# Nine groups of tiles per run of q times k^T v, with one slot in a lent PSUM bank, and k^T v joined to the first run of a later batch

## The chip, the cores and the metric

The kernel runs on one core of one Trainium2 chip. The metric is the device time of one execution in microseconds (us), the median of several runs. "Profiled execution" is one more execution, recorded instruction by instruction; every duration below comes from it.

## The reference, cut to what matters

Linear attention without softmax, an RMS norm, and a gated feed-forward layer, all in float32:

```python
kv  = einsum('bhsd,bhse->bhde', k, v)        # 8 batches, 8 heads, 576 positions, 64 wide
out = einsum('bhsd,bhde->bhse', q, kv)
x   = out / sqrt(mean(out * out, -1) + 1e-6) * g_norm     # then (B,H,S,D) -> (4608, 512)
y   = (1 / (1 + exp(-(x @ w_gate))) * (x @ w_val)) @ w_out  # 512 -> 1536 -> 512
```

`moe_w_gate`, `moe_w_val`, `moe_w_out` arrive as float64 and are converted on the chip.

## The kernel before

**Feed-forward part.** The 4608 rows are nine chunks of 512. Chunk 0 is multiplied plainly (L599, L833). In this time the weights are converted on VectorE and ScalarE in steps named CV (L197 to L237), five to a unit of weights, and a unit of w_out must be ready before the matmuls of L833 that read it. Chunks 1 to 8 use a fast scheme: per chunk 3 x 26 "products" of 128x128 by 128x256 for the first layer (L957, two matmuls to a product) and 26 for the second (L1059). Products go into five PSUM banks, handed out by the queue `free` and returned by `give`. A bank is a *region* with a letter (A to K): several products accumulate into it one after the other, and between them its value is read out, by ScalarE where a step says "o5=A" (L923), by VectorE where it adds (L927). So the next product into a letter waits for the step that reads it out. In the first layer the products 0 to 8 of each third go into A, B, C, E, A, C, B, A, C; "o5=A" stands behind product 3, "o4=C" behind 4, "o3=B o1=A" behind 5.

**Attention part.** Batch 0 is done ahead by `attention`. Batches 1 to 7 are done by `feed(b)` in small steps set between the matmuls of the feed-forward part. For each batch:

- `kv_mm` computes k^T v for all eight heads: 32 matmuls of 128 rows by 64 columns (L389, "mains", positions 0 to 511) and eight of 64 by 64 (L396, "tails", the last 64 positions); `kv_copy` brings the result to `kvq` on ScalarE (L404, L405).
- `turn` transposes q on VectorE (L408, L410) into `qTs`.
- A *run* (`heads_run(m)`, m = 0, 1) is four heads. Its `u_mm` multiplies q by k^T v in 64x64 tiles (L439), four at a time: two halves of the rows of the array (heads g) by two halves of its columns (heads e). Then on ScalarE the square (L444, "sq") and the root (L450), sums on VectorE (L447), the norm, and transposes and DMAs of the result to `xT_ring`.

A run has nine slots for each g. Eight slots fill a PSUM bank, so g = 0 writes the first bank of the tile `at` (three banks, one buffer), g = 1 the second, and both ninth slots lie in the third. Before, the last slot of g = 1 is computed from the other half of the rows, so that the two halves never write one bank together. That takes a second copy of half of k^T v (L405), a second load of the last slots of q (L120) and their transposes (L410), and it makes ten groups: eight with four matmuls, two with two.

A matmul of float32 shows in the trace as two passes, each with a weight load: a run is 36 matmuls and 72 passes.

**Order.** Steps sit at positions: in chunk 0 by the table `places` (88 matmuls; "au" is `u_mm` of batch 1's first run, "bu" of its second, asq and bsq their squares, as0 a sum, LL2 the loads of batch 2's k and v, KV2 its `kv_mm`, ASIDE the copy that frees `at`, D its `kv_copy`); in the chunks 1 to 6 by `where`, position 26 j + i for product i of third j ("25:u0" is `u_mm` of run 0 behind product 25, "54:u1" that of run 1, "56:q1" its square). Every engine works through its own instructions in this order. ScalarE also issues DMAs: of LL2 and of the later k and v loads the four of the last 64 positions (L139).

Of the kernel before, what the change touches and what calls it, by code (L numbers as in the profile page):

```python
# [20 lines left out]
def kernel(  # L21
# [11 lines left out]
    nc = tc.nc  # L33
# [20 lines left out]
    JR = S // QB  # L54
    NSL = JR // 2
    NRUN = NHP // 2
    QW = 2 * S + 2 * HD

    NK4 = S // P
    S4 = P * NK4  # L60
# [44 lines left out]
    def load_q_run(b, m):  # L105
        if b >= B:
            return
        if b == 1:
            t = h_main[2 - m].rearrange("p s c -> p (s c)")[:, 4 * NT * P - QW:4 * NT * P]
        else:  # L110
            t = sb.tile([P, QW], FP32, tag="q", name="q", bufs=1)
        main = t[:, 0:2 * S].rearrange("p (e j c) -> p e j c", e=2, c=QB)
        more = t[:, 2 * S:QW].rearrange("p (e j c) -> p e j c", e=2, c=QB)
        queue = nc.gpsimd if b == 1 else nc.sync
        for i in range(NC):
            for e in range(2):
                for g in range(2):
                    src = q[b, 4 * m + 2 * g + e].rearrange("(p j) d -> p j d", j=JR)[:, :, QB * i:QB * i + QB]
                    queue.dma_start(out=main[HD * g + QB * i:HD * g + QB * i + QB, e], in_=src)
                queue.dma_start(out=more[QB * i:QB * i + QB, e], in_=src[:, JR - 2:JR])  # L120
        q_late[b, m] = t

    kv_late = {}
# [142 lines left out]
    g_col = const.tile([P, 1], FP32, name="g_col")  # L266


    kvq = const.tile([P, 2, NRUN, 2, HD], FP32, name="kvq")
    kv_ahead = const.tile([P, NRUN, 2, HD], FP32, name="kv_ahead")  # L270

    qTs = const.tile([P, QW], FP32, name="qTs")
# [17 lines left out]
    def attention(n, at_ps):  # L290

        b, m = divmod(n, NHP)
        d = {}
        kv = kvq[:, 0, m // 2, m % 2]

        def kv_mm():
            d["kv"] = ps = at_ps("kv")
# [78 lines left out]
    def feed(b):  # L376

        d = {}

        def kv_mm():  # L380

            mains, rest = kv_late[b]
            d["kv"] = ps = at_ps()[:, 0:NRUN, 0:2 * HD].rearrange("p m (e d) -> p m e d", d=HD)
            for m in range(NRUN):
                for e in range(2):
                    for j in range(NK4):
                        for g in range(2):
                            c = slice(NK4 * HD * e + HD * j, NK4 * HD * e + HD * j + HD)
                            nc.tensor.matmul(ps[HD * g:HD * g + HD, m, e], mains[2 * m + g, "k"][:, c],  # L389
                                             mains[2 * m + g, "v"][:, c],  # L390
                                             start=(e == 0 and j == 0), stop=False, skip_group_check=True)
            for e in range(2):
                for m in range(NRUN):
                    for g in range(2):
                        rs, c = slice(PH * m, PH * m + PH), HD * (2 * g + e)
                        nc.tensor.matmul(ps[HD * g:HD * g + HD, m, e], rest[rs, c:c + HD],  # L396
                                         rest[rs, GH + c:GH + c + HD], start=False, stop=True, skip_group_check=True)

        def kv_set_aside():
            nc.scalar.copy(out=kv_ahead, in_=d["kv"])  # L400
            d["kv"] = kv_ahead

        def kv_copy():
            nc.scalar.copy(out=kvq[:, 0], in_=d["kv"])  # L404
            nc.scalar.copy(out=kvq[0:HD, 1], in_=d["kv"][HD:P])  # L405

        def turn(m, e):
            nc.vector.transpose(qTs[:, S * e:S * e + S], q_late[b, m][:, S * e:S * e + S])  # L408
            if e == 1:
                nc.vector.transpose(qTs[0:HD, 2 * S:QW], q_late[b, m][0:HD, 2 * S:QW])  # L410
                if b > 1:
                    load_q_run(b + (m + 1) // NRUN, (m + 1) % NRUN)
                elif m == NRUN - 1:
                    load_q_run(b + 1, 0)

        def heads_run(m):
# [6 lines left out]
            def place(g, s_):  # L423
                return (NSL - 1) * g + s_ if s_ < NSL - 1 else 2 * (NSL - 1) + g
# [2 lines left out]
            def by_head(t):  # L427
                return t.rearrange("p (n d) -> p n d", d=HD)

            def u_mm():  # L430
                d["u"] = u = at_ps().rearrange("p r c -> p (r c)")[:, 0:2 * S]
                for t in range(NSL + 1):
                    for g in range(2):
                        if t < NSL - 1 or g == 0:
                            head, s_ = (1, NSL - 1) if t == NSL else (g, t)
                            o = HD * place(head, s_)
                            for e in range(2):
                                c = 2 * S + HD * e if t == NSL else S * e + HD * s_
                                nc.tensor.matmul(u[HD * e:HD * e + HD, o:o + HD],  # L439
                                                 qTs[HD * g:HD * g + HD, c:c + HD],  # L440
                                                 kvq[HD * g:HD * g + HD, t == NSL, m, e], start=True, stop=True)

            def u_square():
                nc.scalar.activation(out=sq, in_=d["u"], func=AF.Square)  # L444
# [43 lines left out]
            return ([u_mm, u_square, lambda: u_sum(0), lambda: u_sum(1), u_root] + norms +  # L488
                    [lambda i=i: x_turn(i) for i in range(NC)])

        kv = [kv_mm, kv_copy, kv_set_aside] if b == 2 else [kv_mm, kv_copy]
        t0, t1 = ([lambda m=m, e=e: turn(m, e) for e in range(2)] for m in range(NRUN))
        u0, u1 = heads_run(0), heads_run(1)
        if b == 1:
            return kv, t0 + t1 + u0 + u1, ()
        n_ = "n{0}0 n{0}1 n{0}2 n{0}3 n{0}4 n{0}5 n{0}6" if b == 2 else "n{0}0 n{0}1"
# [1 line left out]
        steps_ = dict(zip(names, t0 + t1 + u0 + u1[:-2]))  # L498
        where = """0:t00 5:t01 25:u0 26:q0 28:t10 30:s00,s01 33:t11 35:r0 36:n00 37:n01 39:n02 40:n03 42:n04 43:n05 44:n06
                   51:x00 52:x01 53:u1 56:q1 57:s10,s11 60:r1 62:n10,n11 63:n12 65:n13 66:n14 68:n15 69:n16""" if b == 2 else """  # L500
                   5:t00 8:t01 28:u0 29:t10 30:q0 33:s00,s01 36:r0 39:t11 41:n00 47:n01 51:x00,x01 54:u1
                   56:q1,s10,s11 61:r1 64:n10 66:n11""" if b == 3 else """
                   3:t00 7:t01 28:u0,t10 30:q0,s00,s01 37:r0 39:t11 47:n00,n01 53:x00,x01 54:u1
                   56:q1,s10,s11 60:r1 61:n10 63:n11"""
        first = [(int(w_.split(":")[0]), steps_[x]) for w_ in where.split() for x in w_.split(":")[1].split(",")]
        return kv, first, u1[-2:]
# [53 lines left out]
    def bank(i):  # L560
        return (psum_mm if i < 2 else psum).tile([P, 512], FP32, tag=f"mm{i}", name="mm")
# [6 lines left out]
    def at_ps():  # L568
        return psum.tile([P, NAT, 512], FP32, tag="at", name="at")
# [212 lines left out]
    def w1_form(c, j, part, v):  # L782
        if c == 1:
# [10 lines left out]
    w1_more[1] = [more[:, i] for i in range(10, 18)] + [sgs[-1][:, GH * i:GH * i + GH] for i in range(2)]  # L794
    spare_sg = sgs.pop()
    batch1, second_batch = feed(1), feed(2)
    named = {"LL": lambda: load_late(1), "LL2": lambda: load_late(2), "KV": batch1[0][0], "KV2": second_batch[0][0],
             "W0": lambda: w1_sums(0), "W1": lambda: w1_sums(1),
             "ASIDE": second_batch[0][2], "CV": convert_step}
    named.update({"C": batch1[0][1], "D": second_batch[0][1]})  # L800
    for i in range(NRUN):
        named[f"Q{i}"] = lambda i=i: load_q_run(1, i)
        named.update({f"t{i}{e}": batch1[1][2 * i + e] for e in range(2)})
    for i, which in enumerate("ab"):
        for n, step in enumerate(("u", "sq", "s0", "s1", "rt", "rc", "n0", "n1", "n2", "x0", "x1")):
            named[which + step] = batch1[1][2 * NRUN + 11 * i + n]
    places = """
        1:CV,CV 2:CV,Q0 4:CV,CV 5:CV,CV 6:CV,LL 7:CV,CV 10:CV,CV 11:Q1 15:CV 16:CV,CV 17:t00
        18:CV,CV 19:t01 20:KV 22:CV,CV,C 25:CV 26:CV,CV 29:au,LL2 30:CV
        31:asq 32:CV,t10,as0 34:CV,as1,art 35:CV 36:t11,arc,an0 37:an1 38:CV,an2 40:CV,CV 41:CV,ax0  # L810
        43:ax1 44:KV2,ASIDE 46:CV,W0 47:bu 48:CV,CV,bsq 50:CV,bs0 52:CV,CV 54:bs1 55:CV,CV,brt,D 57:CV,CV 58:CV 60:CV,brc
        62:bn0,bn1 63:bn2 64:CV 65:CV,CV,CV 66:CV,CV 67:CV 71:bx0 72:CV 74:W1 75:bx1
        80:CV,CV,CV,CV,CV 84:CV 87:CV,CV
    """
# [317 lines left out]
    for c in range(1, NG):  # L1132
        at1, at2 = {}, {}
        for p, step in x_late:
            at1.setdefault(p, []).append(step)
        x_late = []
        if c + 1 < B:
            kv, first_, then = second_batch if c == 1 else feed(c + 1)
            for p, step in (list(zip((21, 22) if c == 2 else (19, 20), kv)) if c > 1 else []) + first_:
                at1.setdefault(p, []).append(step)  # L1140
            for p, step in zip((3, 6) if c == 1 else (4, 6), then):
                at2.setdefault(p, []).append(step)
        if c + 1 < NG:
            for n, p in enumerate(X1 if c == 1 else X2 if c + 1 < B else X3):
                step = lambda n=n, c=c: x_sum(c + 1, n)
                if p < NPR:
                    at2.setdefault(p, []).append(step)
                else:
                    x_late.append((p - NPR, step))
        if c == 1:  # L1150
            for at_, forms in ((at1, ((28, 9, 0), (30, 10, 0), (34, 12, 0), (52, 11, 1), (57, 14, 0), (58, 8, 1), (61, 19, 0), (64, 16, 1))), (at2, ((1, 13, 0), (2, 22, 0), (3, 23, 1), (4, 25, 1), (9, 15, 0), (10, 24, 0), (10, 20, 0), (11, 17, 0), (12, 18, 0), (13, 21, 0)))):
                for p, n, pool_ in forms:
                    at_.setdefault(p, []).append(lambda n=n, eng=nc.gpsimd if pool_ else nc.vector, at_once=at_ is at1 or n == 13: w_form(n, eng, at_once))
        first_layer_fast(c, at1)
        if c == 1:
            sgs += [spare_sg] + more_sgs
        second_layer_fast(c, at2)
# [30 lines left out]
```

## Time and profile before

| | us |
|---|---|
| median of three runs (1003.74 to 1005.06) | 1004.05 |
| profiled execution | 1004.44 |
| its span, first to last instruction | 1002.7 |
| outside the span (difference of the two) | 1.7 |
| PE busy | 993.8 (99%) |
| DVE busy | 722.1 (72%) |
| POOL busy | 617.5 (62%) |
| ACT busy | 342.5 (34%) |

PE is TensorE's matmuls, DVE VectorE, ACT ScalarE, POOL GpSimd; PEld are weight loads. The granted TensorE clock is 1.0. In the chain of waits and in the timeline each line is a start, a length, and an engine with the line of the kernel; square brackets tell how long the engine idled before and what released it.

### The profile page before, as it was taken

How to read it: one execution, taken by the hardware profiler on the slowest of the kernel's cores; microseconds unless marked ns; L12 is line 12 of the kernel's file. 1: busy time of each engine (PE TensorE's matmuls, PEld its weight loads, DVE VectorE, ACT ScalarE, POOL GpSimd, SP SyncE). 2: the span in 40 equal slices, each digit the busy share in tenths (PEclk: the TensorE clock that was granted, in tenths of full speed). 3: DMA queues.
4: the chain of work that ended last, by engine and by line, in shares of the span. 5: the costliest groups of instructions: out<-in, count | busy, mean ns of one | idle time of the engine just before them, and what ended most of it. 6: DMA issues, size and time to landing. Idle time of an engine off the chain costs nothing.

```text
span 1002.7 us, 16624 instructions
## 1 busy us (share of the span) xinstructions
PE 993.8 (99%) x5958; PEld 815.8 (81%) x5958; DVE 722.1 (72%) x1198; ACT 342.5 (34%) x606; POOL 617.5 (62%) x988
## 2 busy tenths in 40 slices
PE   8999999999999999999999999999999999999998
PEld 7455447888888888888888888888888888888887
DVE  4989999889757756784677676866587566755672
ACT  4566332562144213530344124421342133213320
POOL 1509997798359633965186707861595449744963
PEclk9999999999999999999999999999999999999999
DMA  9995414673799568846875577755864555444514
GB/s 271 269 265 183 172 51 115 215 236 127 248 301 272 176 189 240 239 156 203 257 240 171 181 223 237 203 171 179 258 201 141 167 173 211 156 149 162 214 53 122
DMA packets 156114, 195.43 MB, mean 195 GB/s; under 512 B 84832, under 2 KB 128864, under 8 KB 156032
## 3 DMA queue, kind: packets, MB, share of 16 engines
q0 software_dynamic: 22000, 114.11, 34.4%
q1 hardware_dynamic: 126864, 78.16, 27.6%
q10 hardware_dynamic: 7168, 2.10, 0.9%
q8 instruction: 47, 0.77, 0.3%
q14 instruction: 35, 0.29, 0.1%
HBM read 160.50 MB, written 25.56 MB: 186 GB/s over the span
## 4 chain that ended last, share of the span: by engine, by line
PE 73%; POOL 2%; DMA 1%; issue 0%; SPq 0%; DVE 0%; POOLq 0%
PE mm L957 46%; PE mm L1059 24%; PE at L439 1%; POOL h L733 1%; PE at L389 1%; DMA h_more<-in_v_dram 1%; POOL w_ring L1030 0%; POOL h_more L733 0%; PE at L396 0%; SPq L134 0%; POOL w L780 0%; DVE sg L927 0%; POOLq L780 0%; POOLq L1030 0%
## 5 line engine op out<-in xcount | busy, mean ns | idle before, releaser
L957 PE MATMUL mm<-xs,w 128*128 128x256 f32 x1428 | 331.8, 380 | 0.0
L957 PEld LDWEIGHTS mm<-xs,w 128*128 128x128 f32 x1428 | 270.5, 190 | 37.1
L957 PE MATMUL mm<-xT,w 128*128 128x256 f32 x948 | 229.8, 380 | 0.0
L957 PEld LDWEIGHTS mm<-xT,w 128*128 128x128 f32 x948 | 179.5, 190 | 25.0 <-issue 0.5
L780 POOL DMA_DIRECT2D w<-kept x84 | 46.8, 557 | 189.4 <-PE mm L957 187.3
L927 DVE TENSOR_TENSOR sg<-sg,mm 128x512 f32<-128x512 f32 (+1 forms) x176 | 100.7, 599 | 85.5 <-PE mm L957 41.5
L1059 PE MATMUL mm<-w,h 128*128 128x256 f32 x630 | 143.1, 379 | 0.3 <-POOL h L733 0.3
L1059 PEld LDWEIGHTS mm<-w,h 128*128 128x128 f32 x630 | 119.6, 190 | 17.0 <-POOL h L733 0.7
L919 POOL TENSOR_TENSOR h<-h,sg 128x512 f32<-128x512 f32 x72 | 96.0, 1350 | 57.0 <-DVE h L927 31.0
L923 ACT COPY temps<-mm 128x512 f32<-128x512 f32 (+1 forms) x128 | 66.0, 538 | 186.9 <-PE mm L1059 94.7
L733 POOL TENSOR_TENSOR h<-h 128x128 f32<-128x128 f32 x216 | 112.1, 531 | 16.6 <-DVE h_more L733 13.1
L1059 PE MATMUL mm<-w,h_more 128*128 128x256 f32 x474 | 108.2, 379 | 0.0
L916 ACT ACTIVATE sg<-sg 128x512 f32<-128x512 f32 x96 | 59.7, 630 | 131.5 <-DVE sg L927 131.5
L1059 PEld LDWEIGHTS mm<-w,h_more 128*128 128x128 f32 x474 | 90.1, 190 | 12.2
L923 ACT COPY sg<-mm 128x512 f32<-128x512 f32 (+1 forms) x112 | 56.9, 510 | 86.5 <-PE mm L1059 45.0
L733 POOL TENSOR_TENSOR h_more<-h 128x128 f32<-128x128 f32 x120 | 61.6, 517 | 34.3 <-DVE h L919 30.0
L927 DVE TENSOR_TENSOR temps<-temps,mm 128x512 f32<-128x512 f32 (+1 forms) x96 | 59.4, 619 | 25.9 <-PE mm L1059 16.6
L599 PE MATMUL mm<-xT,w 128*128 128x512 f32 x176 | 77.8, 596 | 0.1
L927 DVE TENSOR_TENSOR temps<-mm,temps 128x512 f32<-128x512 f32 (+1 forms) x64 | 39.8, 622 | 50.9 <-PE mm L1059 23.6
L923 ACT COPY h<-mm 128x512 f32<-128x512 f32 x48 | 28.1, 585 | 140.4 <-PE mm L957 126.4
L927 DVE TENSOR_TENSOR sg<-mm,sg 128x512 f32<-128x512 f32 (+1 forms) x64 | 39.7, 620 | 45.1 <-PE mm L957 24.5
L599 PEld LDWEIGHTS mm<-xT,w 128*128 128x128 f32 x176 | 32.6, 190 | 39.2 <-issue 36.8
(145 smaller groups left out, 1284.2 us busy)
## 6 DMA issues: line engine op xcount, KB each, us to landing
w<-kept POOLq DMA_DIRECT2D x42, 896.0 KB, 5.7
w<-kept POOLq DMA_DIRECT2D x90, 384.0 KB, 4.6
w<-kept POOLq DMA_DIRECT2D x42, 768.0 KB, 5.5
out_dram<-sg SPq DMA_DIRECT2D x119, 64.0 KB, 1.7
h_more<-in_k_dram SPq DMA_DIRECT2D x28, 256.0 KB, 5.6
h_more<-in_v_dram SPq DMA_DIRECT2D x28, 256.0 KB, 6.5
q<-in_q_dram SPq DMA_DIRECT2D x96, 72.0 KB, 5.0
xT<-xTs SPq DMA_DIRECT2D x96, 72.0 KB, 4.4
```

The source lines that it names most:

```text
L389: nc.tensor.matmul(ps[HD * g:HD * g + HD, m, e], mains[2 * m + g, "k"][:, c], mains[2 * m + g, "v"][:, c], start=(e == 0 and j == 0), stop ...
L439: nc.tensor.matmul(u[HD * e:HD * e + HD, o:o + HD], qTs[HD * g:HD * g + HD, c:c + HD], kvq[HD * g:HD * g + HD, t == NSL, m, e], start=True ...
L599: nc.tensor.matmul(self.ps[i], w[("wg", "wv")[i], self.f][:, m, :], xT[self.c][:, m, :], start=(m == 0), stop=(m == NMT - 1), skip_group_c ...
L733: ops.append((eng, lambda v=v, x=x, sign=sign, y=y, eng=eng: eng.tensor_tensor(out=h_form(v, j), in0=h_form(x, j), in1=h_form(y, j), op=op ...
L780: nc.gpsimd.dma_start(out=granule(g)[:, 0:n], in_=kept1[g // NPA % N3, g % NPA][:, 0:n])
L916: nc.scalar.activation(out=o["o" + step[1]], in_=o["o" + step[1]], func=AF.Sigmoid)
L919: mult.tensor_tensor(out=o[x], in0=o[x], in1=o[y], op=ALU.mult)
L923: nc.scalar.copy(out=o[out_], in_=o[expr])
L927: tt(out=o[out_], in0=o[x], in1=o[y], op=ALU.add if sign == "+" else ALU.subtract)
L957: nc.tensor.matmul(regions[name][1][:, g], ws[:, g], xf[c][wv], start=(new and g == 0), stop=True, skip_group_check=True)
L1059: nc.tensor.matmul(regions[name][1], h_form(hv, j), ws[:, j], start=(used[i] and j == 0), stop=(j == N3 - 1), skip_group_check=True)
```

## The change

- `u_mm` takes a bank out of `free` (bank 4 in chunk 0) for the ninth slot of g = 1. The run then has nine groups of four matmuls, all of the same form. Behind them ScalarE copies the slot, 128x64, from the lent bank to its place in `at`, and the bank is given back.
- The second copy of k^T v, the second loads of q (four DMAs of twelve per run) and their transposes go.
- For batches 3 to 7, `kv_mm` and `kv_copy` no longer stand at products 19 and 20 (21 and 22 for batch 3), nor u0 at 28: all stand behind product 25, in one go. k^T v of run 0 lies in the third bank of `at`, that of run 1 in the lent bank. The tails come first, then the mains of run 0, then those of run 1; each half has a copy of its own.
- Batch 2's `kv_mm` joins "bu" in the same way, at 44 of chunk 0; bu was at 47. Its copy aside is two copies and moves from 44 to 47, behind bsq, which moves from 48 to 47.

```diff
-    QW = 2 * S + 2 * HD
+    QW = 2 * S
...
-                queue.dma_start(out=more[QB * i:QB * i + QB, e], in_=src[:, JR - 2:JR])
...
-        def kv_mm():
+        def kv_mm(at, lent):
             mains, rest = kv_late[b]
+            if at is None:
+                at = at_ps()
+                d["kv"] = ps = [at[:, m, 0:2 * HD]... for m in range(NRUN)]
+            else:
+                d["kv"] = ps = [t... for t in (at[:, NAT - 1, 2 * HD:4 * HD], lent[:, HD:3 * HD])]
+            if b > 2:
+                tails(True)
             for m in range(NRUN):
...
+            if b < 3:
+                tails(False)
...
         def kv_copy():
-            nc.scalar.copy(out=kvq[:, 0], in_=d["kv"])
-            nc.scalar.copy(out=kvq[0:HD, 1], in_=d["kv"][HD:P])
+            for m in range(NRUN):
+                nc.scalar.copy(out=kvq[:, m], in_=d["kv"][m])
...
-                nc.vector.transpose(qTs[0:HD, 2 * S:QW], q_late[b, m][0:HD, 2 * S:QW])
...
+            def u_mm(first=()):
+                at = at_ps()
+                d["u"] = u = at.rearrange("p r c -> p (r c)")[:, 0:2 * S]
+                i_ = 4 if b == 1 else free.popleft()
+                lent = bank(i_)
+                for step in first:
+                    step(at, lent)
+                for s_ in range(NSL):
                     for g in range(2):
+                        o = HD * place(g, s_)
+                        to = lent[:, 0:HD] if s_ == NSL - 1 and g == 1 else u[:, o:o + HD]
+                        for e in range(2):
+                            c = S * e + HD * s_
+                            nc.tensor.matmul(to[HD * e:HD * e + HD], qTs[HD * g:HD * g + HD, c:c + HD],
+                                             kvq[HD * g:HD * g + HD, m, e], start=True, stop=True)
+                nc.scalar.copy(out=u[:, o:o + HD], in_=lent[:, 0:HD])
+                if b > 1:
+                    give(i_)
...
+            u0[0] = lambda u_mm=u0[0]: u_mm((kv_mm, lambda at, lent: kv_copy()))
...
-                   5:t00 8:t01 28:u0 29:t10 30:q0 ...   3:t00 7:t01 28:u0,t10 30:q0,s00,s01 ...
+                   5:t00 8:t01 25:u0 29:t10 30:q0 ...   3:t00 7:t01 25:u0 28:t10 30:q0,s00,s01 ...
...
-        43:ax1 44:KV2,ASIDE 46:CV,W0 47:bu 48:CV,CV,bsq 50:CV,bs0 ...
+        43:ax1 44:bu 46:CV,W0 47:bsq,ASIDE 48:CV,CV 50:CV,bs0 ...
...
-            for p, step in (list(zip((21, 22) if c == 2 else (19, 20), kv)) if c > 1 else []) + first_:
+            for p, step in first_:
```

## The prediction

> **What bounds the kernel now.** I read the page first, then the chain of waits, the waits of PE, and the timelines of PE, ACT and DVE around the insertions.
>
> ```profile
> PE 993.8 (99%) x5958; PEld 815.8 (81%) x5958; DVE 722.1 (72%) x1198; ACT 342.5 (34%) x606; POOL 617.5 (62%) x988
> ```
>
> PE is the bound. The chain shows one batch as PE sees it:
>
> ```profile
> 283.31 0.14 issue
> 283.44 1.12 PE at L389 x30
> ...
> 370.18 17.27 PE mm L957 x80
> 387.45 2.02 PE at L389 x64
> 389.46 0.39 PE at L396 x16
> 389.85 7.97 PE mm L957 x36
> 397.82 1.31 PE at L439 x72
> 399.13 22.64 PE mm L957 x104
> 421.78 1.31 PE at L439 x72
> ```
>
> Nothing stands between insertions and products, so a PE step saved here is time saved. Only batch 3's L389 (283.44) hung on a DMA. PE's waits name a second bound:
>
> ```profile
> PE mm L833 <- DVE w L237: 0.7, 3, 0.4
> ```
>
> At 116.06, 123.38 and 130.67, at the end of chunk 0, PE waits for converted weights. What PE saves before 116 is lost there, and what DVE loses PE loses too.
>
> **Removed: a group of tiles.** L396 takes 16 passes, four rounds of four, in 0.39 us; L439 takes 72 in 1.31, twenty rounds. So a round is (1.31 - 0.39)/16 = 0.058 us (single instructions: 58.3 ns, also where a round holds two matmuls), a group of two passes 0.117. Twelve runs lie in chunks 1 to 6: -1.40. The two of chunk 0 are counted below.
>
> **Moved: k^T v next to u0.** From the starts of single passes in the timeline, beyond PE's steady step (216 ns for a pass of products): entering costs 93 ns, leaving 90 and 104 more for the first pass after, a new form 92 to 94 between, the first round of each form 49. From the last pass before to the second pass after, KV takes 3.036 us and a run 1.941; less two passes (0.432), 2.604 and 1.509: 4.113. Joined: 0.093 to enter, tails 0.243, change 0.150, mains 1.862, change 0.152, nine groups 1.060, leaving 0.148 and 0.104: 3.812. That is 0.301 less, 0.117 of it the group: 0.184 for each of five batches, **-0.92**. Position 25 is 3.4 us behind 21, so batch 3's DMA stall goes: its KV took 3.549 instead of 3.036, **-0.51**.
>
> Does u0 wait for the copy of k^T v? The mains of run 0 end (last start) 0.93 us, 16 rounds, before those of run 1. A copy on ACT starts 0.285 us after the last matmul's start (389.64 to 389.92); a 128x128 copy takes 0.27 (L364). So half 0 is ready about 0.56 after its last start, 0.53 before PE gets to u0 (0.93 + 0.15): nothing, if PE waits for that half alone. Half 1 is ready 0.40 us after u0 would start; only the ninth slots need its banks, 0.98 us into the run. Neither is seen in the trace; bounds: nothing to (0.40 + 0.05) x 5 = 2.3. I take nothing, since PE's mains of batch 3 started on the first pairs of one tile, h_more, while a later pair was still landing. KV off 19 and 20 pulls POOL and DVE nowhere: POOL's first write to h_more came 5.7 us behind product 25 (400.71), k^T v is done 2.4 behind it.
>
> **Added: a copy on ACT at the end of each run.** A 64-column copy takes 0.232 us (L364); the next can start about 0.11 behind its start (0.155 behind a 128-column one, less 64 columns at 0.84 ns, from L923's 585 ns for 512 columns and 372 for 256). What matters is that it stands in ACT's order at u1's place and waits for the end of the run, with "o5=A" and "o4=C" behind it. Before:
>
> ```profile
> 420.14 0.58 ACT L923 COPY h<-mm 128x512 f32<-128x512 f32 x1 [0.73 <-PE mm L957]
> 421.81 0.59 ACT L923 COPY h<-mm 128x512 f32<-128x512 f32 x1 [1.09 <-PE mm L957]
> 423.18 1.13 ACT L444 ACTIVATE sqs<-at 128x1152 f32<-128x1152 f32 x1 [0.78 <-PE at L439]
> 424.21 0.58 ACT L923 COPY sg<-mm 128x512 f32<-128x512 f32 x1
> ```
>
> The first two lines are o5=A and o4=C: they ran before and during the run (421.71 to 423.0), while ACT was free, then the square, then o3=B. Afterwards: the lent copy at 423.06 (0.117 earlier end), o5=A 423.17 to 423.75, o4=C from 423.65, square from 424.13, o3=B 425.16 to 425.74. PE wants A again at 423.87 and B at 425.60, with weight loads 0.21 earlier. After a wait PE resumes 0.05 behind the releaser and its first pass costs 0.104 more (253.21 to 253.27, then 0.320 to the next pass). So A is 0.04 late, then B: 425.74 + 0.05 + 0.10 against 425.64, 0.26. Together 0.30 for each of five u1 at 54: **+1.5**. Ends: nothing (ACT 0.25 quicker) and 0.45 (copy's full 0.23 before the next): 0 to 2.2. u1 of batch 2 stands one product earlier (53), and its A is wanted 0.9 us after o5=A: nothing. u0 at 25 has no product of its third before it, and o5=A waits for product 26 anyway: nothing; its o3=B is ready about 0.1 us in time.
>
> The Trainium skill, "TensorEngine Tiling (Array Packing)", section PSUM Bottleneck, says that packing tiles speeds up TensorE but not the emptying of PSUM, which can become the limit, and advises to share it between ScalarE and VectorE. The trace has ACT busy 34% on the whole, so by totals no such limit; whether it holds at every run is the last rival.
>
> **Chunk 0, where the same copy meets DMA issues.** ACT's order at "au" is copy, four DMAs of LL2, then asq. Now:
>
> ```profile
> 57.97 0.65 ACTq L139 DMA_DIRECT2D h_more<-in_k_dram  x1
> 58.13 1.13 ACT L217 ACTIVATE cz<-cz,exp_off 128x1024 int32<-128x1024 uint32 x1
> 58.71 0.62 ACTq L139 DMA_DIRECT2D h_more<-in_k_dram  x1
> 60.15 2.15 ACTq L139 DMA_DIRECT2D h_more<-in_v_dram  x2
> 62.35 1.13 ACT L444 ACTIVATE sqs<-at 128x1152 f32<-128x1152 f32 x1 [3.08 <-DMA h_more<-in_k_dram]
> ```
> ```profile
> 61.53 0.78 DVE L408 STREAM_TRANSPOSE qTs<-h 128x576 f32<-128x576 f32 x1 [0.91 <-PE at L439]
> 63.51 0.76 DVE L447 TENSOR_REDUCE ms<-sqs 128x9 f32<-128x576 f32 x1 [1.20 <-ACT sqs L444]
> ```
>
> The DMAs were issued while the run was still ahead (it ended at 61.5), and even so the square started late behind the last of them. With the copy in front, which starts at 61.58, all four come behind it: 0.65 + 0.62 + 0.61 + 0.60, with 0.29 of semaphores ahead and 0.06 between, to 64.5. The square moves from 62.35 to 64.55, the sum on DVE by as much, **2.2 us**. Behind the sum DVE has conversions, sums and transposes in one row; its only longer idle time, 70.0 to 72.0, waits for ACT's L217, which hangs on the same chain, and from 83 to past 148 it has no gap but 0.43 at 92, behind ACT. So the delay reaches the three waits at L833. The two transposes of L410 (0.26 each) go, but DVE waits for ACT behind them: nothing. At bu the copy puts L202 behind the run (77.52 to 78.2), yet with 2.2 us of delay the L202 waits for DVE later still; asq's successors then cost about 0.3, and D, now two copies of half the width, gives 0.25 back at the wait at 92. "bu" with KV2 saves PE 0.46, au 0.12; DVE being the bound, these count for nothing. Chunk 0: **+2.2**. Ends: -0.6 (DVE catches up all of it, PE keeps its 0.58) and +2.6.
>
> Eight fewer DMAs on POOL (L120, 0.58 each, 30 to 41 us) and four fewer per run on SP are on nobody's path: POOL then waits until 75.4. POOL's 0.33 at 253 starts from DVE sums that move with PE: nothing either way, at most 0.6.
>
> **Sum.** -1.40 - 0.92 - 0.51 + 1.5 + 2.2 = +0.87 us: the profiled execution from 1004.44 to 1005.3 (span 1002.7 to 1003.6), the median, 0.39 below it, from 1004.05 to **1004.9**. Within 0.2% (2.0 us, about what a measurement of this kernel can tell from no change) that is no change, on the slow side.
>
> **Rivals.**
> - *ACT late nowhere.* DVE catches up in chunk 0 and u1's readers come in time: -0.58 - 2.83 = -3.4, 1000.6. For it: ACT idles two thirds of the time; against it: ACT keeps its order, as at 62.35. 0.11. Half of this (chunk 0 harmless, u1 at its price): -1.9, 1002.1, 0.11; half of it counts as faster.
> - *PE waits for both halves of k^T v at u0.* Five times at the joined insertion, 0.45 each: +2.3, 1007.2, slower. It decides if PE's first matmul of u0 waits for the second copy, that is, idles more than the 0.15 of the change of form. Against it: the pairs of h_more above. 0.16.
> - *PSUM's emptying late at every run.* If all twelve runs from chunk 1 on pay 0.30 instead of five: +2.1, 1007.0, slower. For it: o3=B has only 0.1 us to spare at u0; against it: the other rooms, 0.9. 0.08.
> - *The ninth slot doesn't run beside the others* (18 rounds become 20): +1.4, 1006.3. Against it: different banks and the same form as the other groups. 0.04.
>
> **How the numbers follow.** The forecast has 0.50, with 1003.0 to 1006.5 as its own range; 0.42 of it within 0.2%, 0.07 above, 0.01 below. Faster: 0.11 + 0.055 + 0.01, about 0.18. Slower: 0.07 + 0.16 + 0.08 + 0.04 = 0.35. Same: 0.42 + 0.055, 0.47. The range 1001.8 to 1007.4 holds the forecast and all rivals but the first, and the ends of single costs.
>
> **What would show it.** Right: 72 passes of a run in 1.19 us; a joined insertion of 4.24 us from pass to pass, with no wait of PE on ACT within; waits of PE at L957 on ACT's L923 four and six products into the last third, about 0.3 us, five times; the first L444 near 64.5 and L833's first pass near 118. Wrong: L444 near 62 and L833 before 116; no waits of PE behind u1; a gap of PE at u0 ended by ACT's copy to kvq.

## The result, and the profile after

The changed kernel takes 1008.33 us (median, 1007.13 to 1010.92), the kernel before 1004.05 in the same series. The ratio is 1.0036, with a 95% interval of 1.0025 to 1.0048: 0.36% slower. The profiled execution takes 1008.1 us with a span of 1006.3. The forecast, 1004.9 with a range up to 1007.4, was too low.

From the page, the engine totals and the group of weight loads of the first layer (its last columns are idle time and what ended most of it):

```profile
PE 992.4 (99%) x5958; PEld 813.0 (81%) x5958; DVE 721.7 (72%) x1184; ACT 340.5 (34%) x621; POOL 607.9 (60%) x980
...
L978 PEld LDWEIGHTS mm<-xs,w 128*128 128x128 f32 x1428 | 270.1, 190 | 39.6 <-ACT sg L944 2.0
```

PE is the bound as before, and busy for 1.4 us less. What was added is waiting; most of what the weight loads waited for another engine in this group is the 2.0 us for ScalarE's L944. The chain of waits shows one batch in the changed kernel:

```profile
373.73 22.45 PE mm L978 x104
396.18 0.20 PE at L392 x2
...
396.57 1.08 PE at L403 x32
397.65 0.93 PE mm L403 x32
398.58 1.14 PE at L453 x66
...
399.79 25.23 PE mm L978 x116
425.02 1.14 PE at L453 x66
...
426.23 2.87 PE mm L978 x12
```

k^T v and u0 are one insertion between 396.2 and 399.8 and nothing of another engine stands in it. A run takes 1.21 us (425.02 to 426.23) instead of 1.31. The waits of PE and of its weight loads have these entries that the kernel before had not, or not so large:

```profile
PE at L403 <- ACT sqs L495: 1.4, 1, 1.4
...
PE mm L854 <- DVE w L235: 1.2, 2, 1.0
...
PE mm L619 <- ACT sg L624: 1.0, 1, 1.0
PE at L619 <- DVE w L233: 0.8, 1, 0.8
```
```profile
PEld mm L978 <- ACT sg L944: 2.0, 5, 0.4
```

The first four lie in chunk 0. The last is the forecast wait behind u1, five times. ScalarE around such a u1 (timeline; in brackets the idle time and what ended it):

```profile
426.36 0.20 ACT L455 COPY at<-mm 128x64 f32<-128x64 f32 x1 [3.46 <-PE mm L453]
426.46 1.08 ACT L944 COPY h<-mm 128x512 f32<-128x512 f32 x2
427.42 1.16 ACT L460 ACTIVATE sqs<-at 128x1152 f32<-128x1152 f32 x1
428.44 1.11 ACT L944 COPY sg<-mm 128x512 f32<-128x512 f32 x2
```

It idles 3.46 us in front of the lent copy, with "o5=A" and "o4=C" queued behind it, and "o3=B" comes only at 428.44. PE's gaps there, from one pass to the next, are 301 ns four products into the third and 385 and 320 six products in, against 216 in step: 0.36 us.

Chunk 0, ScalarE and VectorE:

```profile
62.07 0.20 ACT L455 COPY at<-mm 128x64 f32<-128x64 f32 x1 [2.74 <-PE mm L453]
62.38 1.66 ACTq L137 DMA_DIRECT2D h_more<-in_k_dram  x2
64.13 1.27 ACTq L137 DMA_DIRECT2D h_more<-in_v_dram  x2
65.45 1.13 ACT L460 ACTIVATE sqs<-at 128x1152 f32<-128x1152 f32 x1 [3.18 <-DMA st<-in_moe_w_val_dram]
```
```profile
66.61 0.76 DVE L463 TENSOR_REDUCE ms<-sqs 128x9 f32<-128x576 f32 x1 [3.86 <-ACT sqs L460]
...
83.36 0.69 DVE L627 TENSOR_TENSOR h<-mm,sg 128x512 f32<-128x512 f32 x1 [0.22 <-ACT sg L624]
84.40 1.78 DVE L226 SCALAR_TENSOR_TENSOR cz<-st,cz 128x1024 uint32<-128x1024 uint32 x1 [0.34 <-ACT cz L215]
```

The last two lines in the kernel before, where VectorE waited for nothing:

```profile
80.21 0.68 DVE L607 TENSOR_TENSOR h<-mm,sg 128x512 f32<-128x512 f32 x1
80.81 1.21 DVE L228 SCALAR_TENSOR_TENSOR cz<-st,cz 128x1024 uint32<-128x1024 uint32 x1
```

All four DMAs come behind the copy and the square starts at 65.45 instead of 62.35, 0.05 us behind the end of the last issue (the DMA in its bracket is only the last event that the profile found). VectorE is 3.1 us late at 66.61, still 3.1 at the conversion at 79.66 (76.56 before), 3.65 at L233 (86.77 against 83.12), and 4.3 at the last conversion ahead of w_out's first matmul (118.59 against 114.29). Each of these differences holds the 0.38 us by which au starts later in this execution.

Start-up differs between executions (au's first pass lies between 59.4 and 61.7 in the kernels below), so chunk 0 is compared from there on. Call **stretch** the time from au's first pass to the first product of chunk 1: 98.00 us before (60.24 to 158.24), 101.91 after (60.62 to 162.53), 3.91 more. The rest by chunks, from first product to first product: chunk 2 went from 107.15 to 106.59, chunks 3 to 6 from 106.63 to 106.59 each.

### The profile page after: what moved, and what is told of

Read it like the earlier page. It is cut to its first block, busy times and chain, and to the rows that moved or that the text cites. A ratio compares the mean times of both kernels' runs of the same rounds, so it can differ in the third digit from the quotient of the medians.

```text
span 1006.3 us, 16581 instructions
## 1 busy us (share of the span) xinstructions
PE 992.4 (99%) x5958; PEld 813.0 (81%) x5958; DVE 721.7 (72%) x1184; ACT 340.5 (34%) x621; POOL 607.9 (60%) x980
## 4 chain that ended last, share of the span: by engine, by line
PE 74%; POOL 2%; issue 0%; DVE 0%; POOLq 0%
PE mm L978 47%; PE mm L1080 24%; PE at L453 1%; POOL h L753 1%; PE at L403 1%; PE mm L403 0%; POOL w_ring L1051 0%; POOL h_more L753 0%; PE at L392 0%; POOL w L800 0%; DVE sg L948 0%; PE mm L453 0%; PE mm L392 0%; POOLq L800 0%; POOLq L1051 0%
## 5 line engine op out<-in xcount | busy, mean ns | idle before, releaser
L944 ACT COPY temps<-mm 128x512 f32<-128x512 f32 (+1 forms) x128 | 66.6, 546 | 183.5 <-PE mm L1080 94.7
L944 ACT COPY sg<-mm 128x512 f32<-128x512 f32 (+1 forms) x112 | 56.3, 516 | 83.8 <-PE mm L1080 45.0
L619 PE MATMUL mm<-xT,w 128*128 128x512 f32 x176 | 77.8, 596 | 1.1 <-ACT sg L624 1.0
L753 POOL TENSOR_TENSOR h_more<-h 128x128 f32<-128x128 f32 x120 | 57.6, 484 | 34.5 <-DVE h L940 30.2
L948 DVE TENSOR_TENSOR temps<-temps,mm 128x512 f32<-128x512 f32 (+1 forms) x96 | 59.4, 619 | 25.6 <-PE mm L1080 16.6
L944 ACT COPY h<-mm 128x512 f32<-128x512 f32 x48 | 27.7, 588 | 124.1 <-PE mm L978 110.0
L619 PEld LDWEIGHTS mm<-xT,w 128*128 128x128 f32 x176 | 32.6, 190 | 41.0 <-issue 36.1
```

The lines of the kernel that those rows point to most:

```text
L619: nc.tensor.matmul(self.ps[i], w[("wg", "wv")[i], self.f][:, m, :], xT[self.c][:, m, :], start=(m == 0), stop=(m == NMT - 1), skip_group_c ...
L753: ops.append((eng, lambda v=v, x=x, sign=sign, y=y, eng=eng: eng.tensor_tensor(out=h_form(v, j), in0=h_form(x, j), in1=h_form(y, j), op=op ...
L944: nc.scalar.copy(out=o[out_], in_=o[expr])
L948: tt(out=o[out_], in0=o[x], in1=o[y], op=ALU.add if sign == "+" else ALU.subtract)
```

## The experiments

All kernels below in one table; medians stand beside that of the kernel before on the same chip.

| kernel | stretch | chunk 2 | chunks 3 to 6 | median | before | ratio, 95% |
|---|---|---|---|---|---|---|
| before | 98.00 | 107.15 | 106.63 | 1004.05 | | |
| after | 101.91 | 106.59 | 106.59 | 1008.33 | 1004.05 | 1.0036, 1.0025 to 1.0048 |
| ll2_first | 100.12 | 106.59 | 106.59 | 1006.7 | 1005.29 | 1.0012, 1.0 to 1.0024 |
| late_copy | 103.87 | 106.23 | 106.23 | 1006.4 | 1005.29 | 1.0013, 1.0 to 1.0026 |
| both_orders | 100.17 | 106.23 | 106.23 | 1004.42 | 1005.29 | 0.9992, 0.9981 to 1.0003 |
| before_copy | 100.57 | 107.50 | 106.63 | 1007.9 | 1005.29 | 1.002, 1.001 to 1.003 |
| unjoin | 101.89 | 106.78 | 106.78 | 1010.36 | 1005.14 | 1.0042, 1.0027 to 1.0058 |
| swap_copy | 103.69 | 107.19 | 107.19 | 1011.79 | 1005.14 | 1.0062, 1.0043 to 1.0082 |
| old_bu | 100.95 | 106.23 | 106.23 | 1005.6 | 1005.14 | 1.0001, 0.9988 to 1.0014 |
| late_chunk0 | 99.85 | 106.59 | 106.59 | 1005.84 | 1005.31 | 1.0008, 0.9997 to 1.0019 |
| late_all_47 | 100.09 | 106.23 | 106.23 | 1004.44 | 1005.31 | 0.9996, 0.9986 to 1.0007 |
| late_all | 100.11 | 106.23 | 106.23 | 1004.13 | 1005.31 | 0.9988, 0.9974 to 1.0002 |
| old_bu_late | 98.03 | 106.23 | 106.23 | 1002.52 | 1005.31 | 0.9972, 0.9963 to 0.9982 |
| join47 | 98.76 | 106.23 | 106.23 | 1003.65 | 1005.48 | 0.9986, 0.9973 to 0.9999 |
| bu44 | 100.16 | 106.23 | 106.23 | 1004.77 | 1005.48 | 1.0001, 0.9985 to 1.0017 |

In the kernels that move the lent copy the lines behind it are six or seven higher: L625 is L619 of the changed kernel, L630 is L624, L633 is L627, L466 is L460 and L456 is L455.

**ll2_first: the DMAs ahead of the run at au.**

```diff
-        22:CV,CV,C 25:CV 26:CV,CV 29:au,LL2 30:CV
+        22:CV,CV,C 25:CV 26:CV,CV 29:LL2,au 30:CV
```

> The after kernel with one swap: at position 29 of chunk 0 the four DMAs of LL2 stand ahead of au, so on ScalarE they are issued before the lent copy and not behind it. My theory (the copy holds the DMAs up, the DMAs hold asq up, VectorE hands the delay on to L854): the first square (L460) starts near 62.4 instead of 65.45, chunk 1 begins 3 to 4 us earlier (162.5 to about 159), and the time falls from 1008.3 to about 1004.6, all of it in chunk 0. Rival, the rest of chunk 0 (the joined bu, the order of ScalarE behind it, GpSimd's share of the port) is what costs: the square comes early but chunk 1 begins less than 1 us earlier, 1007.5 to 1008.3. Rival, it is no more than the later start of this execution: no change.

The square starts 1.68 us behind au's first pass (63.34 against 61.66) instead of 4.83, and the stretch falls from 101.91 to 100.12: 1.8 us, half of what was expected. So the DMAs behind the copy cost, but 2.1 us of chunk 0's loss stay with the first square on time.

**late_copy: u1's lent copy with its square.**

```diff
-                nc.scalar.copy(out=u[:, o:o + HD], in_=lent[:, 0:HD])
-                if b > 1:
-                    give(i_)
+                def home():
+                    nc.scalar.copy(out=u[:, o:o + HD], in_=lent[:, 0:HD])
+                    if b > 1:
+                        give(i_)
+                d["home"] = home
+                if not (b > 2 and m == 1):
+                    d.pop("home")()
...
             def u_square():
+                if "home" in d:
+                    d.pop("home")()
```

> The after kernel, but for batches 3 to 7 the copy of run 1's ninth slot (and the return of its bank) stands with the square at 56 instead of at 54, so o5=A and o4=C go ahead of it on ScalarE. My theory: the two late passes behind each u1 (0.085 and 0.273 us, five times) go, -1.8 us, 1008.3 to 1006.5, chunks 2 to 6 each 106.2 instead of 106.6 us. Rival: the gaps come from the bank that the ninth slot holds, which is now held longer; then they stay or grow, 1008.3 or more.

Chunks 2 to 6 take 106.23 instead of 106.59: 0.36 each, the whole wait behind u1. Its chunk 0 is the changed kernel's, and yet its stretch is 103.87. The same four DMAs on ScalarE took longer here:

```profile
61.60 0.20 ACT L456 COPY at<-mm 128x64 f32<-128x64 f32 x1 [2.57 <-PE mm L453]
61.91 1.68 ACTq L137 DMA_DIRECT2D h_more<-in_k_dram  x2
63.69 2.26 ACTq L137 DMA_DIRECT2D h_more<-in_v_dram  x2
65.99 1.13 ACT L466 ACTIVATE sqs<-at 128x1152 f32<-128x1152 f32 x1 [4.19 <-DMA h_more<-in_k_dram]
```

The pair for v took 2.26 us instead of 1.27 (in swap_copy 2.08, stretch 103.69; in unjoin 1.27, stretch 101.89). One microsecond more on the queue became nearly two in the stretch. The traces show the second one on PE, at the joined insertion of 44, here in late_copy and then in the changed kernel:

```profile
76.93 1.16 PE L403 MATMUL at<-h_more 128*64 128x64 f32 x31 [2.42 <-ACT sqs L501]
...
77.97 1.86 PE L403 MATMUL mm<-h_more 128*64 128x64 f32 x31
```
```profile
76.37 1.16 PE L403 MATMUL at<-h_more 128*64 128x64 f32 x31 [1.40 <-ACT sqs L495]
...
77.41 1.11 PE L403 MATMUL mm<-h_more 128*64 128x64 f32 x31
```

PE waits 2.42 us there instead of 1.40, and its granted clock is 0.5 from 78.06 to 81.47 us, while it is 1.0 in the changed kernel. The insertion takes 5.02 us (76.93 to 81.95) instead of 3.52. The lent copy and L200 stand behind it on ScalarE, and VectorE waits 1.47 us for L200. In swap_copy it is the same: a wait of 2.21 us, and a clock of 0.5 from 78.62 to 82.04.

**both_orders: the two edits together.**

> Both orders at once: LL2 ahead of au, and the copy of u1 with its square. My theory: the two add up, -3.7 and -1.8 us, 1008.3 to about 1002.8; against the kernel before -0.1 to -0.2%. If only one of the two causes is right, 1004.6 or 1006.5; if neither, 1008.3.

The two add up as each measured alone: stretch 100.17, chunks 106.23, and the time is that of the kernel before. That leaves 2.2 us of chunk 0 unexplained by the prediction.

**before_copy: the kernel before with a lone 64-column copy behind au.**

```diff
+                if b == 1 and m == 0:
+                    nc.scalar.copy(out=kv_ahead[:, 0, 0], in_=u[:, 17 * HD:18 * HD])
```

> The kernel before, with nothing of the change but one more 64-column copy on ScalarE behind au's matmuls (of the last slot, to a place that ASIDE writes later; no result hangs on it). My theory: the first square moves from 62.35 to about 65, VectorE with it, and the time rises by 2.5 to 4 us, 1004.05 to about 1007.3. Rival, that a copy as such costs nothing and chunk 0 loses by the joined bu: no change, below 1004.6.

The copy adds nothing but itself and the delay of the DMAs behind it, and the stretch grows by 2.57 us (100.57), the time by a ratio of 1.002. A copy of 0.2 us costs over 2 us by its place alone.

**unjoin: k^T v of batches 3 to 7 by itself again, at 19 (21).**

```diff
-            u0[0] = lambda u_mm=u0[0]: u_mm((kv_mm, lambda at, lent: kv_copy()))
-            kv = []
+            kv = [lambda: kv_mm(None, None), kv_copy]
...
-            for p, step in first_:
+            for p, step in (list(zip((21, 22) if c == 2 else (19, 20), kv)) if c > 1 else []) + first_:
```

> The changed kernel with the joined insertion of batches 3 to 7 undone: k^T v at 19 (21 for batch 3) with its copies behind it, u0 alone at 25; nine groups, lent copy and chunk 0 stay. By the prediction's working: 0.18 us more in each of five batches (+0.9), and batch 3's k^T v waits for its DMA again (+0.5): +1.4 us against the changed kernel; chunk 2 back from 106.59 to about 107.3, chunks 3 to 6 to 106.77. Rival (the join saves nothing, since its price lies in the changes of form, which stay): chunks 3 to 6 at 106.59 and +0.5 at most.

Each chunk takes 0.19 more, as the prediction's 0.184. But chunk 2 rises by no more than the others: batch 3's wait for its DMA doesn't come back at 21. So the move behind product 25 was not what removed it.

**swap_copy: k^T v's half 1 copied ahead of half 0.**

```diff
-            for m in range(NRUN):
+            for m in (reversed(range(NRUN)) if b > 2 else range(NRUN)):
                 nc.scalar.copy(out=kvq[:, m], in_=d["kv"][m])
```

> The changed kernel with the two copies of k^T v's halves in the other order (half 1 first) for batches 3 to 7. Prices the rival 'PE waits for both halves'. Theory (PE waits for just the half that it reads, and in the changed kernel it came in time): u0 now needs the second copy, some 0.40 us late by the prediction's working: a gap between L403's last pass and L453's first of about 0.55 to 0.65 instead of 0.15, five times, +2.0 to +2.5 us. Rival (PE waited for neither because copies are early, or waits anyway for both): no change against the changed kernel.

From the waits of PE:

```profile
PE at L453 <- ACT kvq L416: 2.7, 5, 0.5
```

Each chunk takes 0.60 more (107.19), all at the start of u0: the gap between the last pass of L403 and the first of L453 is 754 ns instead of 152. In the changed kernel PE thus waits for the half that it reads and no longer. A wait for the second copy would have cost 3.0 us; the order of the copies is what keeps it away.

**old_bu: both_orders with k^T v and bu apart again at 44 and 47.**

```diff
-        43:ax1 44:bu 46:CV,W0 47:bsq,ASIDE 48:CV,CV 50:CV,bs0 ...
+        43:ax1 44:KV2,ASIDE 46:CV,W0 47:bu 48:CV,CV,bsq 50:CV,bs0 ...
```

> both_orders (LL2's DMAs issued ahead of au, late lent copy at u1) with chunk 0's second insertion as in the kernel before: k^T v of batch 2 at 44 with its set-aside, bu alone at 47, its square behind the two conversion steps of 48; bu's run keeps nine groups and the lent copy. Theory (what is left of chunk 0's loss comes from the order on ACT that the joined bu brings: the conversion L200 behind the whole of k^T v and run, square and set-aside ahead of the gate and of L215): DVE's L222 and L226 come back by about 1.5 us, L833's first pass from 118.3 to about 116.1, the first pass of chunk 1 from 160.4 to about 158.3, the time about 2 us below both_orders, some 3 us below the kernel before, although PE has one more insertion (0.46 us) in chunk 0. Rival (the lent copy alone behind bu's run, or the other changes in chunk 0, hold it back): L833 stays near 118 and the time within 0.5 us of both_orders.

The theory fell: the stretch grew to 100.95. ScalarE's timeline shows why:

```profile
77.64 1.16 ACT L200 ACTIVATE w<-w,one 128x1024 f32<-128x1024 uint32 x1
81.39 0.20 ACT L456 COPY at<-mm 128x64 f32<-128x64 f32 x1 [2.58 <-PE mm L453]
81.50 0.60 ACT L630 ACTIVATE sg<-mm 128x512 f32<-128x512 f32 x1
```

L200 is early again, but the lent copy now waits for a run that ends three products later, and the gate L630 behind it, ready long before, waits along (78.57 in the kernel before). VectorE's L633 waits 1.58 us for it. Undoing the place alone laid bare the second cost of the copy.

**act_order: the joined insertion at 46, behind W0.** Its edit overlooks that W0's sums on GpSimd overwrite the tile that holds batch 2's k and v, and stand ahead of the k^T v that reads it here.

```diff
-        43:ax1 44:bu 46:CV,W0 47:bsq,ASIDE 48:CV,CV 50:CV,bs0 ...
+        43:ax1 46:CV,W0,bu 48:CV,CV,bsq,ASIDE 50:CV,bs0 ...
```
```profile
86.60 2.05 PE L403 MATMUL at<-h_more 128*64 128x64 f32 x32 [10.54 <-POOL h_more L777]
```

> both_orders with the joined insertion kept, but moved from 44 to 46, behind the conversion step and W0, and with bu's square and set-aside behind the two conversion steps of 48: ACT's order is then L200, lent copy, conversions, square, set-aside. Theory (only the order on ACT counts, not the join): L200 starts near 77.5 again, before the run, L833's first pass at about 116, the time as old_bu, about 2 us below both_orders. Rival (the joined insertion itself, longer on PE in one piece, delays chunk 0's weights): L833 stays near 118 and the time within 0.5 us of both_orders.

PE waited 10.5 us for those sums; the run (1013.61) decides nothing.

**late_chunk0: the changed kernel with chunk 0's two lent copies at their squares.** As late_copy, with the condition `if b > 1:`.

> The changed kernel with one edit: for batch 1's two runs (chunk 0) the copy of the lent slot is issued right ahead of the square of the run (at 31 behind LL2's DMAs, at 47), not at the end of the run. No place changes, LL2 stays behind au, u1's copies of later batches stay early. Theory A (chunk 0's loss comes from the lent copy's place in ACT's order, where it holds up the DMAs behind au and the conversion L200 behind bu): the first square back within 0.4 us of the run's end as LL2's DMAs go out during it, L200 at 46 ahead of the square again; what is left is square and set-aside at 47 ahead of the gate, about 0.7 us on DVE; chunk 1 starts some 2.5 to 3.5 us earlier than in the changed kernel, the time 1004.5 to 1005.5. Rival B (square and set-aside at 47 ahead of the gate, or the join itself, cost the 2 us that stayed in both_orders): about 1 to 1.5 us from the au side alone, near 1006.5.

Stretch 99.85: with the copy out of the way, the DMAs go out during the run and 2.06 us come back without any place changed. 1.85 us of loss stay.

**late_all_47 and late_all: u1's copies late too, and then bu's square and set-aside behind the conversions of 48.**

```diff
-                if not (b > 2 and m == 1):
+                if b == 2 or (b > 2 and m == 0):
...
-        ... 44:bu 46:CV,W0 47:bsq,ASIDE 48:CV,CV 50:CV,bs0 ...
+        ... 44:bu 46:CV,W0 48:CV,CV,bsq,ASIDE 50:CV,bs0 ...
```

> late_chunk0, and the lent copy of u1 (54) of batches 3 to 7 with its square too: 0.36 us more in each of five chunks (106.23 instead of 106.59), 1.8 us below late_chunk0 by either theory; A: 1002.7 to 1003.7 in all, B: near 1004.7.

> late_all_47 with bu's square (and its lent copy) and the set-aside behind the two conversion steps of 48, as the square stood in the kernel before; the joined insertion stays at 44. A: ACT's order in chunk 0 is that of the kernel before, with two copies more off the path of the conversions; L833's first pass (L854 here) at about 116, chunk 1 starts at about 158.3 (with the same start-up), the time at -0.2 (chunk 0), -0.9 (chunk 2), -0.4 in each of four chunks: 1001.5 to 1002.5. If the order at 47 costs nothing: the same as late_all_47. B (the join itself costs): chunk 1 at 160 or later, 1004.

Both stretches are 100.1, so ScalarE's order at bu is not what is left: in late_all L200, gate and L215 come, counted from au, no later than in the kernel before, and the loss is the same 2.1 us. VectorE of late_all:

```profile
77.17 1.59 DVE L222 SCALAR_TENSOR_TENSOR w<-st,w 128x1024 f32<-128x1024 uint32 x1
80.95 0.69 DVE L633 TENSOR_TENSOR h<-mm,sg 128x512 f32<-128x512 f32 x1 [2.19 <-PE mm L625]
```

It waits for PE: for the last product of a block, matmul 47, which the run at 44 now stands ahead of. In both_orders, with the copy early, the same place had another last wait: L222 waits 1.55 us for L200, which stands behind the lent copy on ScalarE, and L633 then waits 0.36 for the gate and not for PE. So the two waits hide each other, and neither kernel alone shows both.

**old_bu_late: all lent copies late that cost, and k^T v and bu at 44 and 47.**

> old_bu with LL2 back behind au and both lent copies of chunk 0 with their squares: k^T v of batch 2 at 44 alone, bu alone at 47. A: chunk 0 as in the kernel before, chunk 1 at about 158.3, the time as late_all within 0.5 us (the join in chunk 0 is worth nothing while DVE bounds it). B (the join delays chunk 0): below late_all by 1.5 us or more.

The stretch is 98.03, that of the kernel before to 0.03, and the time 1002.52 against 1005.31. VectorE:

```profile
78.21 1.70 DVE L222 SCALAR_TENSOR_TENSOR w<-st,w 128x1024 f32<-128x1024 uint32 x1 [0.65 <-ACT w L200]
79.84 0.68 DVE L633 TENSOR_TENSOR h<-mm,sg 128x512 f32<-128x512 f32 x1
```

L633 finds its product done. late_all and old_bu_late differ in the join and in the place; two more kernels separate them.

**join47: late_all with the joined insertion at 47, W0 behind it. bu44: old_bu_late with bu at 44, not joined.**

```diff
-        43:ax1 44:bu 46:CV,W0 48:CV,CV,bsq,ASIDE 50:CV,bs0 ...
+        43:ax1 46:CV 47:bu,W0 48:CV,CV,bsq,ASIDE 50:CV,bs0 ...
```
```diff
-        43:ax1 44:KV2,ASIDE 46:CV,W0 47:bu 48:CV,CV,bsq 50:CV,bs0 ...
+        43:ax1 44:KV2,ASIDE,bu 46:CV,W0 48:CV,CV,bsq 50:CV,bs0 ...
```

> late_all with the joined insertion of chunk 0 moved from 44 to 47, behind the block's last product; W0's sums, which overwrite the tile that k^T v of batch 2 reads, go behind it. Theory C (what is left of chunk 0's loss is the run's place: at 44 it stands ahead of the products 45 to 47, whose end DVE's L633 waits for, 2.19 us in late_all): L633 waits less than 0.7 us for PE, chunk 0 (first product to first pass of chunk 1) back from 138.25 to 136.1 to 136.8 us (a bit more if GpSimd's sums come late), the time 1.3 to 2.1 us below late_all: 1002 to 1003. Theory D (the joined piece itself, with the longer stretch without products, costs wherever it stands): chunk 0 stays at 138.

> old_bu_late with bu's run moved from 47 to 44, right behind k^T v and the set-aside but not joined with it; its square and lent copy stay behind the conversions of 48. C: L633 on DVE waits about 2 us for PE as in late_all, chunk 0 from 136.14 to about 138, the time 1.5 to 2.2 us above old_bu_late: about 1004.3. D: chunk 0 stays at 136.1, the time as old_bu_late.

VectorE and PE of bu44, then VectorE of join47:

```profile
79.89 1.75 DVE L222 SCALAR_TENSOR_TENSOR w<-st,w 128x1024 f32<-128x1024 uint32 x1 [0.65 <-ACT w L200]
83.02 0.69 DVE L633 TENSOR_TENSOR h<-mm,sg 128x512 f32<-128x512 f32 x1 [1.38 <-PE mm L625]
```
```profile
78.86 1.21 PE L453 MATMUL at<-kvq,qTs 64*64 64x64 f32 x66 [0.55 <-ACT kv_ahead L411]
```
```profile
79.43 0.69 DVE L633 TENSOR_TENSOR h<-mm,sg 128x512 f32<-128x512 f32 x1
```

bu44, without any join, loses 2.16 us (100.16). join47, joined, loses 0.76, and its L633 doesn't wait. So it is the place and not the join. That bu44 loses as much as late_all is in part chance: its run waits 0.55 us for the set-aside copy, and late_all's run has an idle stretch of 0.59 us in it. Nor is all of the loss the wait: counted from au, L633 is 1.49 us later in bu44 than in the kernel before, and another 0.56 comes with L210, which takes 1.24 us at 88.94 instead of 0.68. The 0.76 of join47 likewise comes with longer conversions on VectorE (L233 1.67 us at 82.62, 1.28 before), and with GpSimd's sums, which start at 77.64 instead of 75.39. That the sums are the cause was not tried by itself.

## Why the prediction was wrong, step by step

**The sum, with what each term measured** (from the profiles of before and after unless a run is named):

| term | predicted | measured | from |
|---|---|---|---|
| a group less, 12 runs | -1.40 | -1.24 | a run's insertion 1.941 to 1.838, 0.103 each |
| join, 5 batches | -0.92 | -0.95 | unjoin, 0.19 each |
| batch 3's DMA wait | -0.51 | -0.52 | chunk 2 against chunks 3 to 6 before |
| PE late behind u1, 5 times | +1.5 | +1.8 | late_copy, 0.36 each |
| chunk 0 | +2.2 | +3.91 | stretch |
| sum | +0.87 | +3.0 | |

The two profiled executions differ by 3.66 us; 0.38 of this is start-up ahead of au and 0.29 lies behind chunk 8's last product. The sum closes to 0.01. The medians differ by 4.28 us, 0.62 more than the two profiled executions, and no run shows the cause of that part.

**The step that failed is the term for chunk 0.** The prediction gave it 2.2 us, with an upper end of 2.6, and it measured 3.91. Its mechanism at au was right: copy, four DMAs, square, then VectorE's row of conversions to L854 with hardly any slack. It was sized 2.2; the square came 2.72 us later against au (4.83 instead of 2.11), and alone, in before_copy, the same place cost 2.57. Each of the four issues took what was forecast (0.60 to 0.66 us), but together they took 3.0 us, from 62.38 to 65.4, since 0.37 passed between the first two, for which the prediction had 0.06. In late_copy they took 4.0 and in swap_copy 3.8.

What was taken for next to nothing is bu. The prediction weighed the join at 44 as PE work saved (0.46) that counts for nothing while VectorE is the bound, and on ScalarE it set 0.3 us of cost against 0.25 that D gives back. It had L202 right: in the changed kernel L200 starts at 80.34, when VectorE's L195 ends and not when the copy does. But it did not go through what stands behind it on ScalarE, the gate L624 and L215, nor through what PE hands to VectorE. bu moved from 47 to 44, ahead of products 45 to 47, which stood ahead of it before:

```profile
77.03 2.84 PE L599 MATMUL mm<-xT,w 128*128 128x512 f32 x6
79.80 1.38 PE L439 MATMUL at<-kvq,qTs 64*64 64x64 f32 x72
```

L627 on VectorE, the bound, needs product 47. "PE has time there" is not the same as "PE may be late there". Once au's delay is taken away, the place shows: 1.85 to 2.16 us with the run at 44 and the lent copies late (late_chunk0, late_all_47, late_all, bu44), joined or not, against 0.03 with the run at 47 (old_bu_late).

The two costs overlap: 2.57 and 2.16 alone, 3.91 together. In the changed kernel VectorE enters bu already 2.7 us late, counted from au, so it isn't product 47 that it waits for. Of the 1.2 us that come on top, 0.56 are its waits for ScalarE, where the gate and L215 now stand behind lent copy, L200, square and set-aside; the rest is, on balance, conversions that took longer (L210 at 89.76 took 1.24 us instead of 0.68), and no run shows what made them longer. ScalarE's row there:

```profile
80.11 0.20 ACT L455 COPY at<-mm 128x64 f32<-128x64 f32 x1 [1.88 <-PE mm L453]
80.34 1.15 ACT L200 ACTIVATE w<-w,one 128x1024 f32<-128x1024 uint32 x1
81.40 1.11 ACT L460 ACTIVATE sqs<-at 128x1152 f32<-128x1152 f32 x1
...
82.71 0.62 ACT L624 ACTIVATE sg<-mm 128x512 f32<-128x512 f32 x1
83.20 1.17 ACT L215 ACTIVATE cz<-cz,exp_off 128x1024 int32<-128x1024 uint32 x1
```

The late first square also holds up PE: its norms on ScalarE (L495) hold `at`, for which the joined insertion on PE waits 1.40 us at 76.37. In the changed kernel VectorE isn't made later by this wait. In late_copy and swap_copy, where the square came 1.0 and 0.8 us later still, PE's wait was 2.42 and 2.21 us, the granted clock fell to 0.5 within the insertion, and the stretch grew by 2.0 and 1.8 us. Whether some of the changed kernel's other executions had such a clock, which would raise its median, no run shows.

The Trainium skill, "PSUM — Partial Sum Buffer", section Engine vs sequencer instructions, says that the queues of ScalarE, VectorE and GpSimd are strictly first in, first out. The trace agrees: the gate at 81.50 in old_bu, whose operands were done, started 0.11 us behind the start of the copy that it was queued behind.

**Right.** The joined insertion takes 4.24 us from pass to pass, the run's 72 passes 1.21 (1.19), the gap at u0 is 152 ns, a change of form and no wait, and the waits behind u1 come four and six products into the last third. Each is as forecast; the wait was sized 0.30 and is 0.36.

**Right by number, not by reason.** The DMA wait of batch 3 went, but unjoin shows that the later place isn't needed for it. Both kernels with the old form had it (0.52, and 0.87 in before_copy); no profile of the new form has it. The new form has tails first and four DMAs less in each q load; which of them matters, or whether the issues happened to be shorter, stays open.

**The rivals.** *ACT late nowhere* was wrong in both halves. *PE waits for both halves* was wrong, and swap_copy gives its price: 3.0 us, forecast 2.3. *PSUM's emptying late at every run* was wrong: u0 and batch 2's runs show no wait, only the five u1 of which late_copy removes all 0.36. So the section on the PSUM Bottleneck that was named with it bears on this kernel at a place in ScalarE's order, not as a limit of its throughput. *The ninth slot doesn't run beside the others* was wrong: 72 passes in 1.21 us. The forecast of no change lost by chunk 0. With the measured terms the sum is 3.0 us, a median of about 1007, which is still inside the range up to 1007.4; what took the median past it is the rest of 4.28, that is 0.67 us of start-up and tail and the 0.62 without a known cause. So the range's upper end was missed by more than chunk 0 alone.

**A version that beats both.** old_bu_late keeps nine groups, the lent slot and the join for batches 3 to 7, and moves only when the lent copies are issued and, in chunk 0, k^T v of batch 2 and bu apart again to 44 and 47: 0.9972 of the kernel before (0.9963 to 0.9982). By profile, 1001.85 against 1004.44.

## What to carry to other kernels

When a step is moved on an engine that has time to spare, list what stands between its old place and its new one, and ask who waits for that: three products moved behind a run of 1.2 us cost 1.85 to 2.16 us, though PE was not the bound there. A short instruction that waits for another engine costs what is queued behind it, DMA issues included; put it at the place where its result is needed, not at the end of the step that makes it. When two delays feed one row, measure each alone and both together, since they overlap. When a delay grows on its way through the engines, look at the granted clock of that stretch before you look for a cause in the order.

## What the runs showed of the hardware that was not expected

- Issuing four DMAs from ScalarE held it for 3.0 us in the changed kernel and 4.0 us in late_copy, with the same code: single issues took 0.60 to 0.66 us, but the last one 1.62 in late_copy and 1.38 in swap_copy. The Trainium skill, "DMA: Bandwidth & Descriptors", section Issuing engines are not separate DMA queues, calls the time to initiate a DMA usually small relative to the DMA. The trace agrees, with 2.5 and 5.3 us from issue to landing for such DMAs of k and v (medians in the changed kernel's DMA view); but in before_copy it was the cost, 2.57 us, since compute stood behind the issues.
- In chunk 0 PE was idle ahead of the joined insertion for 1.28 to 1.40 us in before_copy (ahead of its k^T v), unjoin and the changed kernel, and its granted clock stayed at 1.0. After 2.42 us in late_copy and 2.21 in swap_copy it was 0.5 for 3.41 us, beginning 1.13 and 0.36 us behind the restart, and in act_order, with an idle time of 10.5 us, it was 0.5 for 10.24. The 3.41 us made the insertion 1.5 us longer in late_copy.
- In two kernels with the joined insertion at 44 PE idled within the run with nothing to wait for that the profile shows (0.6 us in late_all, 0.9 in late_all_47). Its cause was not settled. late_chunk0 has the same chunk 0 as late_all_47 and no such gap: its L633 waits 1.05 us for PE instead of 2.46, and its stretch is 0.24 shorter (99.85 against 100.09), so little of the gap reaches the stretch.
